# Linear attention and top-1 routing on one core: where the states grow, who zeroes the lists, when the early ranks are taken

## The chip, the cores and the metric

The kernel runs on one core of one Trainium2 chip. The metric is the device time in microseconds (us). A profile of one execution stands beside it; its times count from the start of that execution.

## What is computed

```python
for b in range(nb):                      # blocks of 64 positions
    intra = einsum('bhic,bhjc->bhij', qb, kb) * Dmask
    intra = einsum('bhij,bhjd->bhid', intra, vb)
    inter = einsum('bhid,bhde->bhie', qb * lam_pow, kv_state)
    out[:, :, sl] = intra + inter
    kv_state = lam_block * kv_state + einsum('bhsd,bhse->bhde', kb_dec, vb)
x = out.transpose(0, 2, 1, 3).reshape(B * S, H * D)          # 3072 x 512
expert_idx = argmax(x @ w_gate); gate_w = its softmax value
for e in range(8):
    out[mask] = gate_w[mask, None] * (relu(xe @ w1[e]) @ w2[e])
```

Batch is 4, heads 8, length 768, head size 64. Each of the 3072 tokens goes to one of 8 experts, with a hidden layer of 1024. Everything is float32.

## The kernel before

**Attention.** The kernel works in steps of 128 positions, so there are 6 steps n (`NSTEP`), and in each step it takes two batches b at a time. That makes 12 pairs, (0,0), (0,2), (1,0) and so on to (5,2), called pair 0 to pair 11 below. For a pair the following is done.

- `load` (L89) brings q, k and v of the pair by SyncE's queue. Each has a ring of three buffers. Pair 0 is loaded in halves, one batch at a time, with the decay rates `lam` behind q.
- `turn_qk` (L200) transposes q and k on PE in halves s of four heads (four transposes each for q and for k, in the order q, k, q, k). ScalarE copies the result into `qT` and `kT` (L212, L221). VectorE makes `qsT`, the decayed q, for n > 0, and GpSimd makes `kd`, the decayed k (L227).
- `score` (L232) multiplies `kT` and `qT`, and VectorE multiplies the result by the decay mask into `mt` (L243), one buffer for each half s, from a ring of two (pool `work`).
- `attend_states` (L254) adds what the states give, in two ways: way 0 before attention and way 1 after it. Between way 0 and attention stands the fence (L270): ScalarE copies one column of each of the two outputs, and attention, which adds to the same outputs, has to wait for that copy.
- `attend` (L272) multiplies `mt` and v into banks 6 and 7, 32 matmuls.
- `grow` (L286) multiplies `kd` and v into bank 4, 32 matmuls, for all steps but the last; `update` (L298) adds that to the decayed states.
- `to_sbuf` (L280) copies the outputs into `xT`. In the next iteration `rows` (L310) multiplies them by `back`, an identity with the gate weights beside it. That gives the tokens' rows, which go to the tensor `xs` in HBM, and their gate logits. It uses banks 4 to 7.

**Routing.** `choose` (L328) finds the expert of each token on VectorE. `put` (L360) ranks the tokens on PE (`rank`, bank 5) and GpSimd writes an entry for each token into the experts' lists `slots`, with one indirect write for each batch. Steps 0 to 3 are ranked four batches at a time, steps 4 and 5 two at a time. The lists have to be filled with empty entries first: GpSimd sets the tile `empty` (L383), which takes a buffer of the ring `mt`, and SyncE copies it into `slots` (L627), behind the loads of the first two pairs and eight small loads of the gate weights (L625).

Once batches 0 and 1 of step 4 are ranked, the first 256 places of expert 0's list are final, filled or left empty, and `start_early` (L673) reads them and gathers the rows. The ranks of these two batches are the early ranks. The first pass of the experts (`passes[0]`, list 0a) works on them. `turn` (L446) transposes the gathered rows in 8 transposes (L451); VectorE and ScalarE take turns in emptying the two banks that they use.

**Order.** `pin` (`keep_in_program_order`) keeps an instruction of PE where the program has it; what is not pinned is placed by a scheduler. The main loop (L691) has in each iteration: `leave` (rows and choice of the pair before), `enter` (loads and turn of the pair ahead), the ranks that are due from the iteration before, then this pair's states, attention, growth, second half of the states, and the scores of the pair ahead:

```python
        attend_states(cur, 0)
        attend(cur)
        grow(cur)
        attend_states(cur, 1)
```

After the loop come the transposes of the first pass, the last ranks, the last rows, and the experts: nine passes over lists, from the second on with fewer, larger products and sums on VectorE and GpSimd. The transposes of the first pass are not pinned, so they stand among the last pair's attention.

Of the kernel before, what the change touches and what calls it, by code (L numbers as in the profile page):

```python
# [10 lines left out]
F32 = mybir.dt.float32  # L11
I32 = mybir.dt.int32
# [8 lines left out]
def kernel(  # L21
# [64 lines left out]

    qkv = ctx.enter_context(tc.tile_pool(name="qkv", bufs=3))

    def load(n, b0, per=2, then=None):  # L89

        got = [qkv.tile([P, 2, H, D], F32, tag=name, name=f"{name}_in") for name in "qkv"]
        for t, src in zip(got, (q, k, v)):
            for b in range(0, 2, per):
                nc.sync.dma_start(
                    out=t[:, b:b + per].rearrange("p b h d -> p (b h) d"),
                    in_=src[b0 + b:b0 + b + per, :, n * C:(n + 1) * C, :].rearrange(
                        "b h s d -> s (b h) d"))
            if then and t is got[0]:
                then()
        return got  # L100


# [2 lines left out]
    def load_lam():  # L105
        nc.sync.dma_start(out=lam_bc, in_=lam.partition_broadcast(P))

    loaded = {(0, 0): load(0, 0, 1, load_lam), (0, 2): load(0, 2)}
    ident = const.tile([P, P], F32, name="ident")
    make_identity(nc, ident)  # L110

# [3 lines left out]
    for c in range(DC // 2):  # L115
        nc.gpsimd.tensor_copy(back[:, c, :P], ident)
        nc.gpsimd.tensor_copy(back[:, c, P + 2 * E:W + E + D], ident[:, D:])
        nc.gpsimd.tensor_copy(back[:, c, W + E + D:], ident[:, :D])
    before = const.tile([P, P], F32, name="before")
    make_upper_triangular(nc, before, val=1.0, diag=False)  # L120
    ones = const.tile([P, P], F32, name="ones")
# [67 lines left out]
    def bank(i, shape, name):  # L189
        return ps.tile(shape, F32, tag=f"bank{i}", name=name)  # L190
# [4 lines left out]

    pin = tc.keep_in_program_order

    def turn_qk(m, s):  # L200

        shp = [P, HP // 2, 2, C]

        def turned(src, t):
            for i, j in itertools.product(range(HP // 2), range(2)):
                h = s * HP + 2 * i
                pin(nc.tensor.transpose(t[:, i, j, :], src[:, j, h:h + 2, :], ident))  # L207
            return t

        tq = turned(m.q, bank(2 * s, shp, "tq"))  # L210
# [8 lines left out]
        tk = turned(m.k, bank(2 * s + 1, shp, "tk"))  # L219
# [31 lines left out]
    def out_at(m, b, u, hp):  # L251
        return m.op[b][halves[u ^ (hp & 1)], hp, :]

    def attend_states(m, way):  # L254

        if way == 0:
            m.op = [bank(6 + b, [P, HP, C], f"op{b}") for b in range(2)]
        if m.n > 0:
            for hp, b in itertools.product(range(HP), range(2)):
                u = b ^ way  # L260
                pin(nc.tensor.matmul(  # L261
                    out_at(m, b, u, hp), lhsT=st[halves[u], m.b + b, hp, :],
                    rhs=m.qsT[hp // 2][halves[u], hp % 2, b, :],
                    start=(way == 0 and hp < 2), stop=(way == 1 and hp >= HP - 2),
                    skip_group_check=True))
        if m.n > 0 and way == 0:


            for b in range(2):
                nc.scalar.copy(fence[halves[b ^ 1]], out_at(m, b, b, HP - 1)[:, C - 1:])  # L270

    def attend(m):  # L272
        for hp, b, u in itertools.product(range(HP), range(2), range(2)):
            pin(nc.tensor.matmul(  # L274
                out_at(m, b, u, hp), lhsT=m.v[:, b, 2 * hp + u, :],
                rhs=m.mt[hp // 2][:, u, hp % 2, b, :],
                start=(m.n == 0 and hp == 0), stop=(m.n == 0 and hp == HP - 1),
                skip_group_check=True))
# [81 lines left out]
    def put(n, bs, oh, ohc):  # L360


        nb = len(bs)
        shp = [P, nb, E]
        rank = bank(5, shp, "rank")
        pin(nc.tensor.matmul(rank, lhsT=before, rhs=oh, start=True, stop=False))  # L366
        pin(nc.tensor.matmul(rank, lhsT=ones, rhs=ohc, start=False, stop=True))
        place = small.tile(shp, F32, tag="place", name="place")
        nc.vector.tensor_add(place, rank, base[0].unsqueeze(1).to_broadcast(shp))
        nc.vector.tensor_mul(place, place, oh)  # L370
        slot = small.tile([P, nb], F32, tag="slot", name="slot")
        nc.vector.reduce_sum(slot, place, axis=AX.X)
        slot_i = small.tile([P, nb], I32, tag="slot_i", name="slot_i")
        nc.vector.tensor_copy(slot_i, slot)  # L374
        for i, b in enumerate(bs):
            put = nc.gpsimd.indirect_dma_start(  # L376
                out=slots, out_offset=bass.IndirectOffsetOnAxis(ap=slot_i[:, i:i + 1], axis=0),
                in_=entry[:, n, b, :], in_offset=None)

            tc.declare_no_dep(put.ins, group="put", reason="disjoint rows of the lists")  # L380
            tc.add_to_no_dep_group("put", put.ins)

    empty = work.tile([P, E * R // P, ENTRY], I32, tag="mt", name="empty")  # L383
    nc.gpsimd.memset(empty, 0)
    nc.gpsimd.memset(empty[:, :, 1], N)

# [56 lines left out]
        else:  # L443
            nc.vector.tensor_scalar_max(dst, src, 0.0)

    def turn(m):  # L446
        m.xgT = ffn.tile([P, DC, m.n], F32, tag="xgT", name="xgT", bufs=1)
        for dc in range(DC):
            tp = bank(next(tp_banks), [P, m.n], "tp")
            for t, w in enumerate(m.widths):  # L450
                nc.tensor.transpose(tp[:, t * P:t * P + w],  # L451
                                    m.xg[t // 2][:w, t % 2, dc * P:(dc + 1) * P], ident[:w, :w])
            evac(dc, m.xgT[:, dc, :], tp)

    def hidden(m, w1t):
# [163 lines left out]
                data1=zeros, initial=1.0, op0=ALU.mult, op1=ALU.add)  # L619
        nc.vector.tensor_copy(sdec[:, :, 0], qdec[:, :, C - 1])  # L620

    for c in range(DC // 2):
        for j, half in itertools.product(range(2), range(2)):
            f0 = (2 * c + j) * P + (half ^ j) * D
            nc.sync.dma_start(out=back[halves[half], c, P + j * E:P + (j + 1) * E],  # L625
                              in_=moe_w_gate[f0:f0 + D, :])
    nc.sync.dma_start(out=slots.rearrange("(p r) c -> p (r c)", p=P),  # L627
                      in_=empty.rearrange("p r c -> p (r c)").bitcast(F32))
    nc.sync.dma_start(out=xs[0, :].rearrange("(c p) -> c p", c=DC), in_=zeros[:DC, :])

    groups = ([(n, list(range(B))) for n in range(NSTEP - 2)]
              + [(n, [b, b + 1]) for n in range(NSTEP - 2, NSTEP) for b in range(0, B, 2)])
# [17 lines left out]

    def give_places(*group):
        put(*group)
        if group[:2] == early:
            start_early()
# [60 lines left out]


    cnt = bank(7, [P, E], "cnt")
# [121 lines left out]
```

## Time and profile before

The median of three runs is 502.1 us (500.6 to 502.86). The profiled execution has a span of 497.5 us.

| engine | busy us | share of the span |
|---|---|---|
| PE (matmul) | 465.9 | 94% |
| PEld (weight load) | 390.0 | 78% |
| VectorE (DVE) | 216.6 | 44% |
| ScalarE (ACT) | 129.5 | 26% |
| GpSimd (POOL) | 245.6 | 49% |

In the profile, L12 is line 12 of the kernel; a group's name reads output<-inputs. An entry in square brackets is the idle time of the engine before an instruction and what ended it. "PEclk" is the granted clock of PE in tenths. SPq, ACTq and POOLq are the queues from which SyncE, ScalarE and GpSimd issue transfers. Busy shares are averages over attention (to about 150 us) and the experts (the rest), which have different limits.

| load, from the issues | count | KB each | us to landing, median |
|---|---|---|---|
| q, k, v of a pair | 11 each | 512 | 7.8, 7.7, 9.0 |
| rows into `xs` | 24 | 256 | 4.6 |
| list entries into `slots` | 24 | | 4.3 |
| gather for list 0a | 2 | | 3.5 |

### The profile page before, as it was taken

Reading aid. Unit: us, or ns where it says so; the run is one execution under the profiler, and the core shown is the slowest. Engines: PE = TensorE matmul, PEld = TensorE weight load, DVE = VectorE, ACT = ScalarE, POOL = GpSimd, SP = SyncE. Lnnn points to the kernel's source line nnn. Section 1 sums busy time; section 2 is a strip of 40 time slices with the busy share of each in tenths; the row PEclk is TensorE's granted clock in tenths of the full one; section 3 lists DMA queues with packets and bytes.
Section 4 is the critical chain, followed back from the end, with each engine's and each line's share of the span. In section 5 each row is a group of like instructions: output and inputs, shape, how many; then the busy total and the mean of one; then the engine's idle time right before and its main releaser. Section 6 shows DMA issues by size and latency. Waiting matters only on the chain.

```text
span 497.5 us, 8717 instructions
## 1 busy us (share of the span) xinstructions
PE 465.9 (94%) x3468; PEld 390.0 (78%) x3468; DVE 216.6 (44%) x525; ACT 129.5 (26%) x333; POOL 245.6 (49%) x187
## 2 busy tenths in 40 slices
PE   5399999999969999999999999999999999999994
PEld 4398889889848657795799599589779879869963
DVE  2256565555624013446235524633723623563431
ACT  2144445444412011131212112222212211211210
POOL 5023545254233392985960992496298199531001
PEclk9689999999969999999999999999999999999999
DMA  9899998996121765706061542605326236001001
GB/s 186 163 233 260 226 278 234 300 260 153 46 85 44 253 196 180 260 25 237 28 211 32 202 145 93 233 24 212 131 118 215 90 144 210 22 19 42 1 16 49
DMA packets 99961, 72.85 MB, mean 146 GB/s; under 512 B 81266, under 2 KB 81270, under 8 KB 99912
## 3 DMA queue, kind: packets, MB, share of 16 engines
q1 hardware_dynamic: 91560, 52.96, 38.6%
q0 software_dynamic: 4896, 12.97, 7.2%
q10 hardware_dynamic: 3456, 6.29, 3.5%
q8 instruction: 29, 0.48, 0.4%
q14 instruction: 20, 0.16, 0.1%
HBM read 59.13 MB, written 13.40 MB: 146 GB/s over the span
## 4 chain that ended last, share of the span: by engine, by line
PE 69%; issue 1%; DMA 1%; DVE 1%; POOLq 0%; POOL 0%; ACT 0%
PE p L536 27%; PE p L564 17%; PE po L594 16%; PE ph L460 5%; PE tp L451 3%; DMA xg<-xs,list_0a 1%; PE op L274 1%; PE op L261 0%; DVE h_qsT L483 0%; DVE hT L545 0%; DMA slots<-entry,slot_i 0%; PE tx L316 0%; PE tx L318 0%; POOLq L792 0%; PE rank L366 0%
## 5 line engine op out<-in xcount | busy, mean ns | idle before, releaser
L594 PE MATMUL po<-w2t,hT 128*128 128x512 f32 (+2 forms) x224 | 81.1, 597 | 0.0
L422 POOL DMA_INDIRECT xg<-xs,list x24 | 25.9, 1080 | 75.4 <-PE tp L451 69.9
L594 PEld LDWEIGHTS po<-w2t,hT 128*128 128x128 f32 (+2 forms) x224 | 31.6, 169 | 37.5 <-issue 37.2
L547 ACT ACTIVATE hT<-hT 128x384 f32<-128x384 f32 (+2 forms) x56 | 30.2, 539 | 89.8 <-DVE hT L545 89.8
L428 POOL DMA_INDIRECT out_dram<-o,list x24 | 23.8, 990 | 52.0 <-DVE o L600 28.9
L376 POOL DMA_INDIRECT slots<-entry,slot_i x24 | 23.4, 976 | 46.9 <-DVE slot_i L374 21.6
L227 POOL TENSOR_TENSOR kd<-k_in,kdec 128x512 f32<-128x512 f32 x20 | 20.4, 1042 | 48.2 <-issue 26.3
L536 PE MATMUL p<-xgT,w1t 128*128 128x192 f32 (+2 forms) x224 | 42.8, 334 | 0.0
L536 PEld LDWEIGHTS p<-xgT,w1t 128*128 128x128 f32 x224 | 38.7, 190 | 1.1 <-issue 0.8
L243 DVE TENSOR_TENSOR mt<-sp,decay 128x512 f32<-128x512 f32 x48 | 30.0, 683 | 18.6 <-PE sp L237 10.0
L274 PE MATMUL op<-mt,v_in 128*64 128x128 f32 x384 | 25.9, 292 | 4.9 <-ACT fence L270 4.9
L274 PEld LDWEIGHTS op<-mt,v_in 128*64 128x64 f32 x384 | 23.0, 148 | 8.2 <-ACT fence L270 7.0
L576 DVE SCALAR_TENSOR_TENSOR o<-p,list,o 128x256 f32<-128x256 f32 x28 | 13.6, 484 | 32.9 <-PE p L564 17.0
L207 PE MATMUL tq<-ident,q_in 128*128 128x128 f32 x96 | 16.2, 294 | 12.0 <-DVE mt L243 7.3
L564 PE MATMUL p<-w2t,hT 128*128 128x256 f32 x112 | 26.8, 382 | 0.0
L564 PEld LDWEIGHTS p<-w2t,hT 128*128 128x128 f32 x112 | 21.0, 190 | 6.9 <-issue 4.4
L237 PE MATMUL sp<-qT,kT 64*128 64x128 f32 x384 | 26.3, 290 | 0.0
L451 PEld LDWEIGHTS tp<-ident,xg 128*128 128x128 f32 (+1 forms) x112 | 13.8, 144 | 15.2 <-issue 7.9
L237 PEld LDWEIGHTS sp<-qT,kT 64*128 64x128 f32 x384 | 24.0, 199 | 2.0 <-issue 1.5
L451 PE MATMUL tp<-ident,xg 128*128 128x128 f32 (+1 forms) x112 | 19.8, 288 | 5.8 <-DMA xg<-xs,list_0a 4.8
L460 PE MATMUL ph<-xgT,w1t 128*128 128x256 f32 (+1 forms) x128 | 24.7, 348 | 0.0
L545 DVE TENSOR_TENSOR hT<-p,u_qsT 128x384 f32<-128x384 f32 (+2 forms) x28 | 16.1, 575 | 16.5 <-PE p L536 16.5
(160 smaller groups left out, 946.1 us busy)
## 6 DMA issues: line engine op xcount, KB each, us to landing
w1t<-in_moe_w_dram SPq DMA_DIRECT2D x8, 2048.0 KB, 8.5
w2t<-in_moe_w_dram SPq DMA_DIRECT2D x8, 2048.0 KB, 8.8
xs<-x ACTq DMA_DIRECT2D x24, 256.0 KB, 4.6
q_in<-in_q_dram SPq DMA_DIRECT2D x11, 512.0 KB, 7.8
k_in<-in_k_dram SPq DMA_DIRECT2D x11, 512.0 KB, 7.7
v_in<-in_v_dram SPq DMA_DIRECT2D x11, 512.0 KB, 9.0
q_in<-in_q_dram SPq DMA_DIRECT2D x2, 256.0 KB, 3.5
k_in<-in_k_dram SPq DMA_DIRECT2D x2, 256.0 KB, 4.5
```

The costliest lines, as they stand in the source:

```text
L237: pin(nc.tensor.matmul(sp[u][:, i, b, :], lhsT=m.kT[s][halves[u], i, b, :], rhs=m.qT[s][halves[u], i, b, :], start=(i == 0 and b == 0), st ...
L243: nc.vector.tensor_mul(mt[:, u], sp[u], decay[:, u, s * HP // 2:(s + 1) * HP // 2].unsqueeze(2).to_broadcast(shp))
L274: pin(nc.tensor.matmul(out_at(m, b, u, hp), lhsT=m.v[:, b, 2 * hp + u, :], rhs=m.mt[hp // 2][:, u, hp % 2, b, :], start=(m.n == 0 and hp = ...
L376: put = nc.gpsimd.indirect_dma_start(out=slots, out_offset=bass.IndirectOffsetOnAxis(ap=slot_i[:, i:i + 1], axis=0), in_=entry[:, n, b, :] ...
L422: nc.gpsimd.indirect_dma_start(out=dst, out_offset=None, in_=xs[:rows, :], in_offset=bass.IndirectOffsetOnAxis(ap=idx, axis=0))
L428: put = nc.gpsimd.indirect_dma_start(out=out, out_offset=bass.IndirectOffsetOnAxis(ap=idx, axis=0), in_=src, in_offset=None, bounds_check= ...
L451: nc.tensor.transpose(tp[:, t * P:t * P + w], m.xg[t // 2][:w, t % 2, dc * P:(dc + 1) * P], ident[:w, :w])
L460: nc.tensor.matmul(ph, lhsT=w1t[:, dc, fc * P:(fc + 1) * P], rhs=m.xgT[:, dc, :], start=(dc == 0), stop=(dc == DC - 1))
L536: nc.tensor.matmul(p[:, i, :], lhsT=lhs[:, dc, (c + i) * P:(c + i + 1) * P], rhs=rhs[:, dc, :], start=(dc == 0), stop=(dc == DH - 1))
L547: nc.scalar.activation(outs[i][k], outs[i][k], ACT.Relu)
L564: nc.tensor.matmul(p, lhsT=lhs[:, fc, :], rhs=rhs[:, fc, :], start=(fc == 0), stop=(fc == FC // 2 - 1))
L594: nc.tensor.matmul(po[part], lhsT=m.hT[:, fc, t * P:t * P + w], rhs=w2t[:, fc, :], start=(i < k), stop=(i >= FC - k), skip_group_check=True)
```

## The change

It has five parts.

1. `grow` is called between the first half of the states and attention instead of after attention. It works on another bank, so that PE has something to do while the fence is awaited. The fence is now one column of one output, read by one copy.
2. `empty` moves to a buffer of its own, from the ring `xg`, which the experts use later. The copy into `slots` and the zero row of `xs` are issued by GpSimd instead of SyncE, and the gate weights come in four loads on ScalarE's queue instead of eight on SyncE's, at the start.
3. For pair 0, k is loaded on ScalarE's queue beside q on SyncE's, and the turn has both halves of q first and then both of k.
4. The early ranks are taken right after attention of pair 9, the pair whose iteration chooses them, instead of at the start of the states of pair 10.
5. The transposes of the first pass are pinned behind the last pair's states; the last ranks of all are no longer pinned.

```diff
-            for b in range(0, 2, per):
-                nc.sync.dma_start(
+            queue = nc.scalar if first and src is k else nc.sync
+            for b in range(0, 2, per):
+                queue.dma_start(
...
+    by_chunk = moe_w_gate.rearrange("(c j u d) e -> j u d c e", c=DC // 2, j=2, u=2)
+    for j, u in itertools.product(range(2), range(2)):
+        nc.scalar.dma_start(out=back[(u ^ j) * D:((u ^ j) + 1) * D, :, P + j * E:P + (j + 1) * E],
+                            in_=by_chunk[j, u])
...
-            for b in range(2):
-                nc.scalar.copy(fence[halves[b ^ 1]], out_at(m, b, b, HP - 1)[:, C - 1:])
+            nc.scalar.copy(fence[halves[0]], out_at(m, 1, 1, HP - 1)[:, C - 1:])
...
-        pin(nc.tensor.matmul(rank, lhsT=before, rhs=oh, start=True, stop=False))
-        pin(nc.tensor.matmul(rank, lhsT=ones, rhs=ohc, start=False, stop=True))
+        for lhs, rhs in ((before, oh), (ones, ohc)):
+            mm = nc.tensor.matmul(rank, lhsT=lhs, rhs=rhs, start=(lhs is before),
+                                  stop=(lhs is ones))
+
+            if (n, bs[-1]) != (NSTEP - 1, B - 1):
+                pin(mm)
...
-    empty = work.tile([P, E * R // P, ENTRY], I32, tag="mt", name="empty")
+    empty = ffn.tile([P, E * R // P, ENTRY], I32, tag="xg", name="empty", bufs=2)
...
-    for c in range(DC // 2):
-        for j, half in itertools.product(range(2), range(2)):
-            f0 = (2 * c + j) * P + (half ^ j) * D
-            nc.sync.dma_start(out=back[halves[half], c, P + j * E:P + (j + 1) * E],
-                              in_=moe_w_gate[f0:f0 + D, :])
-    nc.sync.dma_start(out=slots.rearrange("(p r) c -> p (r c)", p=P),
-                      in_=empty.rearrange("p r c -> p (r c)").bitcast(F32))
-    nc.sync.dma_start(out=xs[0, :].rearrange("(c p) -> c p", c=DC), in_=zeros[:DC, :])
+    nc.gpsimd.dma_start(out=slots.rearrange("(p r) c -> p (r c)", p=P),
+                        in_=empty.rearrange("p r c -> p (r c)").bitcast(F32))
+    nc.gpsimd.dma_start(out=xs[0, :].rearrange("(c p) -> c p", c=DC), in_=zeros[:DC, :])
...
-        for s in range(2):
-            turn_qk(m, s)
+
+        for s, turn_one in (((0, turn_q), (1, turn_q), (0, turn_k), (1, turn_k)) if not (n or b)
+                            else ((0, turn_q), (0, turn_k), (1, turn_q), (1, turn_k))):
+            turn_one(m, s)
...
         if due:
-            give_places(*due)
+            give_places(due)
         attend_states(cur, 0)
+        grow(cur)
         attend(cur)
-        grow(cur)
+        if chosen and chosen[0][:2] == early:
+            give_places(chosen.pop())
         attend_states(cur, 1)
...
-    turn(passes[0])
-    if chosen:
-        give_places(*chosen.pop())
+    turn(passes[0], pin)
+    give_places(chosen.pop())
     leave(last)
-    give_places(*chosen.pop())
+    give_places(chosen.pop())
```

More of the change, by code (lines that the diff above doesn't have):

```diff
@@ L87, with load @@
     qkv = ctx.enter_context(tc.tile_pool(name="qkv", bufs=3))
-    def load(n, b0, per=2, then=None):
+    def load(n, b0, first=False):
         got = [qkv.tile([P, 2, H, D], F32, tag=name, name=f"{name}_in") for name in "qkv"]
+        per = 1 if first else 2
         for t, src in zip(got, (q, k, v)):
+            queue = nc.scalar if first and src is k else nc.sync
             for b in range(0, 2, per):
-                nc.sync.dma_start(
+                queue.dma_start(
                     out=t[:, b:b + per].rearrange("p b h d -> p (b h) d"),
@@ L97, in load @@
                         "b h s d -> s (b h) d"))
-            if then and t is got[0]:
-                then()
+            if first and src is q:
+                load_lam()
         return got
@@ L106, in load_lam @@
         nc.sync.dma_start(out=lam_bc, in_=lam.partition_broadcast(P))
-    loaded = {(0, 0): load(0, 0, 1, load_lam), (0, 2): load(0, 2)}
+    loaded = {(0, 0): load(0, 0, True), (0, 2): load(0, 2)}
     ident = const.tile([P, P], F32, name="ident")
@@ L194, with pin, turned, turn_q @@
     halves = [slice(0, D), slice(D, P)]
[L198 to L210, printed above, removed]
+    def pin(inst):
+        tc.keep_in_program_order(inst)
+    turned_shape = [P, HP // 2, 2, C]
+    def turned(src, s, t):
+        for i, b in itertools.product(range(HP // 2), range(2)):
+            h = s * HP + 2 * i
+            pin(nc.tensor.transpose(t[:, i, b, :], src[:, b, h:h + 2, :], ident))
+        return t
+    def turn_q(m, s):
+        shp = turned_shape
+        tq = turned(m.q, s, bank(2 * s, shp, "tq"))
         qT = work.tile(shp, F32, tag="qT", name="qT")
@@ L218, in turn_qk, with turn_k @@
             m.qsT.append(qsT)
-        tk = turned(m.k, bank(2 * s + 1, shp, "tk"))
+    def turn_k(m, s):
+        shp = turned_shape
+        tk = turned(m.k, s, bank(2 * s + 1, shp, "tk"))
         kT = work.tile(shp, F32, tag="kT", name="kT")
@@ L444, in relu, with turn @@
             nc.vector.tensor_scalar_max(dst, src, 0.0)
-    def turn(m):
+    def turn(m, pin=lambda inst: inst):
         m.xgT = ffn.tile([P, DC, m.n], F32, tag="xgT", name="xgT", bufs=1)
@@ L450, in turn @@
             for t, w in enumerate(m.widths):
-                nc.tensor.transpose(tp[:, t * P:t * P + w],
-                                    m.xg[t // 2][:w, t % 2, dc * P:(dc + 1) * P], ident[:w, :w])
+                pin(nc.tensor.transpose(tp[:, t * P:t * P + w],
+                                        m.xg[t // 2][:w, t % 2, dc * P:(dc + 1) * P],
+                                        ident[:w, :w]))
             evac(dc, m.xgT[:, dc, :], tp)
@@ L644, in enter, with give_places @@
         m.q, m.k, m.v = loaded[n, b]
-        for s in range(2):
-            turn_qk(m, s)
+        for s, turn_one in (((0, turn_q), (1, turn_q), (0, turn_k), (1, turn_k)) if not (n or b)
+                            else ((0, turn_q), (0, turn_k), (1, turn_q), (1, turn_k))):
+            turn_one(m, s)
         return m
     chosen = []
-    def give_places(*group):
+    def give_places(group):
         put(*group)
```

## The prediction

> **What bounds the kernel now.** I read the busy tenths first, then PE's waits in the attention stage (0 to 160 us), then the timeline around each long wait, then the chain of waits, and last a table of stretches for the clock.
>
> ```profile
> PE   5399999999969999999999999999999999999994
> PEclk9689999999969999999999999999999999999999
> GB/s 186 163 233 260 226 278 234 300 260 153 46 85 44 253 196 180 260 25 237 28 211 32 202 145 93 233 24 212 131 118 215 90 144 210 22 19 42 1 16 49
> ```
>
> PE is full except in the first two slices (12.4 us each), the twelfth and the last; next to the first and in the twelfth the granted clock dips too. So it is attention, up to about 150 us, that has time to give. The waits (waiting engine and line, releaser: total us, times, longest):
>
> ```profile
> PE tq L207 <- DVE mt L243: 7.3, 1, 7.3
> PE op L274 <- ACT fence L270: 4.9, 9, 1.1
> PE tp L451 <- DMA xg<-xs,list_0a: 4.8, 2, 3.9
> DVE mt L243 <- DMA slots<-empty: 8.6, 1, 8.6
> ```
>
> The first and last are one wait. The timeline (start, us, instruction, idle before it) shows it:
>
> ```profile
> 12.24 6.83 SPq L625 DMA_DIRECT2D back<-in_moe_w_gate_dram  x8
> 19.19 0.52 SPq L627 DMA_DIRECT2D slots<-empty  x1
> 22.33 1.29 DVE L243 TENSOR_TENSOR mt<-sp,decay 128x512 f32<-128x512 f32 x2 [8.56 <-DMA slots<-empty]
> 23.08 1.11 PE L207 MATMUL tq<-ident,q_in 128*128 128x128 f32 x4 [7.30 <-DVE mt L243]
> 24.98 3.17 PE L274 MATMUL op<-mt,v_in 128*64 128x128 f32 x32
> 67.02 1.97 PE L274 MATMUL op<-mt,v_in 128*64 128x128 f32 x32 [1.06 <-ACT fence L270]
> 68.82 1.10 PE L291 MATMUL cp<-v_in,kd 128*64 128x64 f32 x32
> ```
>
> `empty` holds one of the two `mt` buffers until its copy into the lists lands, and that copy stands on SyncE's queue behind eight gate loads. The same 32 matmuls take 3.17 us after the pause and 1.97 in a later pair. The last two lines are the fence: PE waits for it between states and attention, with 1.1 us of growth matmuls standing behind.
>
> The chain of waits begins at the third hole:
>
> ```profile
> 131.98 0.96 DMA slots<-entry,slot_i
> 132.94 5.33 issue
> 138.26 0.28 POOL xg L422
> 138.55 1.00 issue
> 139.54 3.55 DMA xg<-xs,list_0a
> 143.13 0.90 PE tp L451 x3
> ```
>
> List entries, list read, gather, first transpose: 143.13 is set by how early the early ranks come. The stretches (length, busy us of PE, PEld, DVE, ACT, POOL, granted clock, DMA share, GB/s):
>
> ```profile
> 23.08:32.94 9.86, 9.86 (x120) 9.34 (x121) 4.31 (x11) 3.13 (x8) 2.04 (x2) 0.78 1.18 218
> 32.94:128.91 95.97, 91.36 (x1442) 84.76 (x1441) 56.28 (x170) 47.47 (x154) 40.03 (x40) 1.00 0.94 237
> 143.13:168.34 25.21, 25.20 (x162) 21.08 (x163) 9.35 (x57) 5.38 (x19) 7.75 (x9) 0.86 0.23 72
> 168.34:497.50 329.16, 321.32 (x1568) 259.68 (x1567) 136.06 (x242) 64.43 (x131) 185.56 (x108) 1.00 0.35 125
> ```
>
> The slow clock costs 9.86 x 0.22 = 2.2 us after the first hole and 25.21 x 0.14 = 3.5 us after the third. DMA is almost full during attention (0.94, 237 GB/s): there lies the danger.
>
> **What the Trainium skill says.** "TensorE: Matmul & The Clock Gate", Part 1: The HAM clock gate: PE falls to half clock after an idle window of about 3.4 us and needs as long a busy one to recover. The trace agrees (3.17 against 1.97 us, above). "DMA: Bandwidth & Descriptors", Issuing engines are not separate DMA queues: transfers from SyncE, ScalarE and GpSimd share the same engines; moving one saves only issue time. That is 6.83 us of issue here. "ScalarE: Activation LUTs", What ACT_TABLE_LOAD costs: 1283 ns; the trace has 1.28 us.
>
> **The change part by part.** Pairs are numbered 0 to 11.
>
> *Start.* `empty` leaves the `mt` ring, so the second product for pair 0 follows its scores. What then sets PE, step by step:
> - In the changed order ScalarE has two k loads, four gate loads and the table load ahead of its first copy; the third gate load waits for the first half of k, which PE had at 6.63. So the first copy starts at 6.6 + 2 x 0.6 + 1.3 = 9.1 instead of 6.05. Three copies of 0.59 later, at 10.9, the scores start (10.37 before), and end at 14.6 (3.69 us). Price of the move: 0.5 us.
> - Pair 1's k landed at 15.0. Now the zeros (432 KB, issued by GpSimd after its first `kd`, about 9.4 us) share the queue: pair 1's three loads of 0.52 MB landed at 12.6, 15.0 and 17.2, which is 230 GB/s, and 0.44 MB at that rate is 2 us; the earlier issue on SyncE returns about 0.5. So 16.5. No row shows a direct GpSimd copy; its issue lies between 1.0 us (the indirect rows) and 3 us (2.0 + 0.44/0.436, the DMA page's section Anatomy of one DMA, an estimate), and the second `kd` behind it is not due before 18. Hidden.
> - Then three quarter turns (0.6 each), growth 1.1, attention 1.9, scores 2.0, rows 1.95: pair 2's turn starts at 16.5 + 8.8 = 25.3. Its k must be there: pair 1's v at 17.2 + 2, two more loads of 2.25 us: 23.7. It is.
> - Before, that turn started at 32.94. Gain 7.6 (9 if the zeros disturb nothing, 5.6 if PE stays at the slow clock). It contains the 2.2 us of clock.
>
> *Growth between the halves.* Eight waits of pairs 2 to 9 sum to 4.6 us (0.26 to 1.06 each). The 1.1 us of growth now runs while ScalarE does the fence, now one copy, not two. Growth needs bank 4, which ScalarE empties before banks 6 and 7, which the states already await; and `kd`, which GpSimd finished a whole pair earlier even with four list writes (61.2 to 63.2, used at 68.8). Gain 4.4; 0.2 is left for hand-overs. Pairs 10 and 11 have no growth and keep their wait.
>
> *Early ranks in the same pair.* They move from 128.91 to behind attention of pair 9. Counted in times of before: turn of pair 10 ends at 118.35; ranks 0.5, states 0.6, growth 1.0, attention 1.8: about 122.5. Vector work puts the slots at 124, but GpSimd still issues the four writes of the group before (120.2 to 125.0), so the early two go at 125.0 to 127.3 instead of 130.71 to 132.94: 5.7 us earlier. List and gather follow as before: 137.4 instead of 143.1. The wait of `had` for VectorE (0.3) stays.
>
> *End pinned.* The transposes now stand behind the whole attention of pair 11. From 118.35 PE has 11.2 us to the end of pair 10's turn, 7.2 to the end of pair 10's rows, 3.7 for the last pair: it arrives at 140.5, 3 us after the rows. The 4.8 us of idling and the 3.5 us of slow clock go. Against that, nothing lies between the transposes any more: the third needs bank 0 back (0.4 us copy), the fourth a ScalarE copy behind two `xT` copies of 0.54: 0.7 us shown. The DMA is busier at that moment than before (list writes at 77 to 82 us landed after 5.8 us, idle ones after 2.1), so I take 0.5 us of waiting on average. Gain 4.8 + 3.5 - 0.7 - 0.5 = 7.1.
>
> *Moved along.* The other list writes in two pieces and the `xg` ring turned by one lie beside PE. The experts' 329 us run unchanged; the gather for the second pass landed at 173.4 and was used at 182: hidden as before.
>
> Sum: 7.6 + 4.4 + 7.1 = 19.1. 502.1 - 19.1 = 483.0.
>
> **The rivals.**
> - *The loads become the bound.* For it: 28.5 MB must land before the last attention (18.9 of q, k and v, 4.2 of weights, 5.0 of rows written, 0.4 of zeros). From 25 us on the seven full slices have 256 GB/s on average; with 5.2 MB landed by 26 the other 23.3 take 91 us, to 117; PE now wants the last pair about 12 us earlier (127.2 - 12 = 115). Against it: k and q of the last pair lie ahead of the second weight load, and before the change no pair after the second waited. If it came, half of start and fences (6) and 3 of the end would be lost: 492.
> - *The early list is late.* Writes and gather run into the last weight load, each landing 3 to 4 us later as above: about 8 us, PE pauses 5 us and cools again (3): 491.
> - *Slower.* Three queues cut each other down to, say, 200 GB/s (181 in the first stretch): 28.5/0.2 = 142 us, the last pair starts at 143 instead of 127.2; 16 lost, 7 gained at the end: 511.
>
> **How the numbers follow.** Forecast 0.75, loads 0.12, late list 0.08, slower 0.05. The likeliest gives 483. Its own bounds are 5.6 to 9 at the start, 4 to 4.6 for the fences, 4 to 8.3 at the end: 480 to 488.5. The range reaches down for a run or two of spread (500.6 to 502.86) and up to the two rivals: 477 to 491. Faster by over 0.5% (2.5 us) holds in all but the last case: 0.93; same 0.02.
>
> **What would show it.** No wait of a `mt` product for the zeros; pair 2's turn near 25; no fence wait over 0.1 us in pairs 2 to 9; early list writes right behind the four before them; transposes behind the last states, at 128 to 129, at full clock; the experts' stretch still 329 us. Wrong would be: PE waiting for q_in or k_in after pair 2, a gather landing after the last states, ScalarE's first copy after 10, or pair periods that stay at 10.6 us.

## The result and the profile after

| | median us | lowest to highest | runs |
|---|---|---|---|
| before | 501.72 | 500.60 to 502.86 | 4 |
| after | 478.49 | 477.37 to 478.98 | 4 |

The ratio is 0.9534, with a 95% interval of 0.9506 to 0.9562: 23.2 us or 4.6% faster. 483.0 was forecast, so the kernel gained 4 us more than the steps promised. The profiled execution of after has a span of 477.2 us (497.5 before), PE is busy for 457.3 us of it (465.9), 96%.

The busy tenths of after, as shown for before, 40 slices of the span:

```profile
PE   4799999999899999999999999999999999999994
PEclk9999999999999999999999999999999999999998
GB/s 170 240 243 260 217 239 216 257 305 279 101 47 320 157 193 250 32 243 33 208 13 242 36 212 87 157 199 47 243 110 132 233 39 211 0 19 44 1 17 51
```

The hole in the twelfth slice is gone, the second slice is fuller (7 for 3), and the granted clock no longer dips. The third row stays high without a break to the tenth slice and ends there: the last load of attention, pair 11's v, lands at 123.1 us.

PE's waits between 0 and 150 us (engine and line, releaser: us in all, times, longest):

```profile
PE tq L213 <- DMA q_in<-in_q_dram: 6.8, 2, 4.8
...
PE tp L465 <- DMA xg<-xs,list_0a: 1.3, 1, 1.3
PE tq L213 <- DVE mt L254: 1.1, 1, 1.1
PE op L284 <- ACT fence L280: 0.4, 2, 0.2
```

The first row is mostly the load of the very first q, 4.84 us, which before had too (4.17). The 7.3 us for an `mt` product are down to 1.1, and these are no longer a wait for zeros: VectorE's `mt` now waits for nothing but the scores. The ten fences cost 0.4 us in place of 4.9 (the two left are in pairs 10 and 11, which have no growth to put between), and the gather 1.3 in place of 4.8.

The start in the timeline of after (start, us, instruction, idle before it):

```profile
15.75 0.63 PE L213 MATMUL tk<-ident,k_in 128*128 128x128 f32 x4 [1.45 <-DMA k_in<-in_k_dram]
...
18.16 1.92 PE L284 MATMUL op<-mt,v_in 128*64 128x128 f32 x32
23.95 0.60 PE L213 MATMUL tq<-ident,q_in 128*128 128x128 f32 x4
```

Pair 1's k sets the pace at 15.75, as the prediction had it (16.5), and pair 2's turn, the last line, comes at 23.95 and not at 32.94. Attention of pair 0, the line between, takes 1.92 us, not 3.17: the clock stayed full through this wait and the 1.1 us before it.

The chain of waits that ended last begins, in after, with:

```profile
112.81 0.97 POOL slots L390
113.78 10.63 issue
...
125.70 3.79 DMA xg<-xs,list_0a
```

That is the same chain as before (list entries, list read, gather). The entry comes 19 us earlier (131.98) but the gather only 14 (139.54), since the line between them has grown from 5.33 to 10.63 us. We come back to it. What it costs PE is one entry of the timeline, at the transposes:

```profile
129.53 0.55 PE L465 MATMUL tp<-ident,xg 128*128 128x128 f32 x3 [1.27 <-DMA xg<-xs,list_0a]
```

And the stretches of after (length, busy us of PE, PEld, DVE, ACT, POOL, clock, DMA share, GB/s). They are pair 3's turn to the early ranks, and the experts:

```profile
33.06:108.45 75.39, 75.39 (x1234) 69.76 (x1232) 52.98 (x149) 37.29 (x119) 34.23 (x34) 1.00 1.02 248
...
148.08:477.20 329.12, 321.32 (x1569) 259.70 (x1567) 135.96 (x242) 64.51 (x131) 185.43 (x108) 1.00 0.35 125
```

In the first line PE is busy for all of its 75.39 us, where before had 4.6 us of fence waits in the like stretch. The last line is the experts' 329.16 us of before, untouched.

Cutting both traces at the same events (starts of turns, and the start of the first output product) tells where the 20.3 us between the two profiled spans came from:

| stretch | before | after | saved | forecast |
|---|---|---|---|---|
| start to pair 2's turn | 32.94 | 23.95 | 9.0 | 7.6 |
| pair 2's turn to pair 3's | 9.14 | 9.11 | 0.0 | in the next |
| pair 3's turn to pair 10's | 74.52 | 69.76 | 4.8 | 4.4 |
| pair 10's turn to the first output product | 51.57 | 45.10 | 6.5 | 7.1 |
| the rest | 329.30 | 329.27 | 0.0 | 0 |

The medians lie 23.2 us apart, 3 us more than these spans. The profiled execution of before took 499.25 us, 2.5 less than its median, and that of after 478.98, 0.5 more than its own. So some of what the change removes is probably larger in an ordinary execution of before than in the one profiled; the experiments below show which waits can vary.

### The profile page after: what moved, and what is told of

Same layout as the page of the kernel before. It is cut to its first block, busy times and chain, and to the rows that moved or that the text cites. A ratio compares the mean times of both kernels' runs of the same rounds, so it can differ in the third digit from the quotient of the medians.

```text
span 477.2 us, 8695 instructions
## 1 busy us (share of the span) xinstructions
PE 457.3 (96%) x3468; PEld 383.1 (80%) x3468; DVE 224.4 (47%) x525; ACT 127.0 (27%) x323; POOL 247.7 (52%) x189
## 4 chain that ended last, share of the span: by engine, by line
PE 71%; issue 3%; DVE 1%; DMA 1%; POOL 0%; POOLq 0%; ACT 0%
PE p L551 28%; PE p L579 18%; PE po L609 16%; PE ph L475 5%; PE tp L465 3%; DMA xg<-xs,list_0a 1%; DVE h_qsT L498 0%; DVE hT L560 0%; PE tx L326 0%; POOL slots L390 0%; PE tx L328 0%; DVE xgT L452 0%; PE rank L377 0%; POOLq L805 0%; ACT hT L562 0%
## 5 line engine op out<-in xcount | busy, mean ns | idle before, releaser
L390 POOL DMA_INDIRECT slots<-entry,slot_i x24 | 23.6, 985 | 34.9 <-DVE slot_i L388 13.7
L591 DVE SCALAR_TENSOR_TENSOR o<-p,list,o 128x256 f32<-128x256 f32 x28 | 13.5, 483 | 32.9 <-PE p L579 17.0
L248 PE MATMUL sp<-qT,kT 64*128 64x128 f32 x384 | 24.7, 278 | 0.1
L248 PEld LDWEIGHTS sp<-qT,kT 64*128 64x128 f32 x384 | 22.4, 188 | 2.2 <-issue 1.9
L284 PE MATMUL op<-mt,v_in 128*64 128x128 f32 x384 | 23.6, 274 | 0.4 <-ACT fence L280 0.4
L560 DVE TENSOR_TENSOR hT<-p,u_qsT 128x384 f32<-128x384 f32 (+2 forms) x28 | 16.1, 575 | 16.5 <-PE p L551 16.5
L293 ACT COPY xT<-op 128x512 f32<-128x512 f32 x24 | 12.9, 590 | 33.6 <-PE op L272 29.8
L488 DVE TENSOR_TENSOR u_kT<-p,u_qT 128x384 f32<-128x384 f32 (+2 forms) x14 | 8.1, 576 | 29.3 <-PE p L551 29.3
```

The source lines that it names most:

```text
L248: pin(nc.tensor.matmul(sp[u][:, i, b, :], lhsT=m.kT[s][halves[u], i, b, :], rhs=m.qT[s][halves[u], i, b, :], start=(i == 0 and b == 0), st ...
L284: pin(nc.tensor.matmul(out_at(m, b, u, hp), lhsT=m.v[:, b, 2 * hp + u, :], rhs=m.mt[hp // 2][:, u, hp % 2, b, :], start=(m.n == 0 and hp = ...
L390: put = nc.gpsimd.indirect_dma_start(out=slots, out_offset=bass.IndirectOffsetOnAxis(ap=slot_i[:, i:i + 1], axis=0), in_=entry[:, n, b, :] ...
```

## Experiments

**Theory.** The change is three separate savings at three places in attention, each about as large as its holes in the trace, and they add up. **Rivals.** The own buffer does all of the start and moving the queues nothing. Fences that vanish come back as waits for loads, which are full. At the end one of early ranks and pinning is idle, or the list writes behind the weight load take back what the early ranks win.

There were twelve runs, each with a profile. The first four stand beside the kernel before at 501.09 us (median of 7), the next four beside 513.57 (median of 11), on a chip where the same kernel takes longer, and the last four beside 501.33 (median of 11). Each is compared with its own kernel before; two kernels are compared with each other only within one of these groups.

### One part alone

**The buffer alone.** The kernel before with one line changed, so that the zeros get their own buffer but stay on SyncE's queue:

```diff
-    empty = work.tile([P, E * R // P, ENTRY], I32, tag="mt", name="empty")
+    empty = ffn.tile([P, E * R // P, ENTRY], I32, tag="xg", name="empty", bufs=2)
```

> The kernel before with one edit: the empty entries get their own buffer; SyncE still issues the gate loads and the zeros. If the queues matter too (my theory), PE's 7.3 us wait for the product goes, but the loads of pair 2 are still issued at 20.2 us behind the gate loads; its k lands at about 27, so pair 2's turn starts near 27.3 instead of 32.9: 5.6 us less than before. If the buffer was all (rival), the turn starts near 24 as in the changed kernel: 9 us less.

Measured: 495.71 us (494.00 to 496.63), ratio 0.9885 (0.9840 to 0.9931), 5.4 us faster. The timeline of this kernel shows where the rest of the start went:

```profile
20.92 0.39 SPq L94 DMA_DIRECT2D q_in<-in_q_dram  x1
25.69 0.63 PE L207 MATMUL tq<-ident,q_in 128*128 128x128 f32 x4 [2.05 <-DMA q_in<-in_q_dram]
28.51 1.09 PE L207 MATMUL tk<-ident,k_in 128*128 128x128 f32 x4 [2.19 <-DMA k_in<-in_k_dram]
```

Pair 2's loads now stand behind the eight gate loads, which SyncE issues from 12.50 to 19.81, and the zeros. Its q is issued at 20.92 and PE waits 2.05 us for it, then 2.19 for its k, and after that PE is at half clock (1.09 us for the four transposes instead of 0.63). Pair 3's turn comes at 38.06: 4.0 us earlier than before, where the whole change brings 9.0. So the wait for the buffer hid a second one behind it, that for loads that stand late in the queue.

**The whole start.** Parts 2 and 3 of the change, nothing else; beside the buffer, these lines:

```diff
-    for c in range(DC // 2):
-        for j, half in itertools.product(range(2), range(2)):
...
-    nc.sync.dma_start(out=slots.rearrange("(p r) c -> p (r c)", p=P),
+    nc.gpsimd.dma_start(out=slots.rearrange("(p r) c -> p (r c)", p=P),
...
+            queue = nc.scalar if first and src is k else nc.sync
...
+        nc.scalar.dma_start(out=back[(u ^ j) * D:((u ^ j) + 1) * D, :, P + j * E:P + (j + 1) * E],
```

> The kernel before with the whole start of the change (own buffer, zeros by GpSimd, gate weights and the first k on ScalarE's queue, all of q turned first) and nothing else. Theory, the parts add up: pair 2's turn at 24.0, 9.0 us less than before in time. Rival, the loads become the bound once PE is earlier: PE waits for q_in or k_in in later pairs and the gain is 6 us or less.

Measured: 492.28 us (489.73 to 494.29), ratio 0.9824 (0.9774 to 0.9874), 8.8 us faster. Pair 3's turn comes at 33.03, as in after (33.06). Of the 8.8 us the buffer alone had 5.4; the other 3.4 are the three moves between queues and the new order of the turn, taken together (the two kernels' intervals overlap a little; in the two profiles pair 3's turn lies 5.0 us apart). One of the moves is taken back by itself further down.

**Growth alone.** Part 1:

```diff
-            for b in range(2):
-                nc.scalar.copy(fence[halves[b ^ 1]], out_at(m, b, b, HP - 1)[:, C - 1:])
+            nc.scalar.copy(fence[halves[0]], out_at(m, 1, 1, HP - 1)[:, C - 1:])
...
         attend_states(cur, 0)
-        attend(cur)
         grow(cur)
+        attend(cur)
```

> The kernel before with growth between the first half of the states and attention, and one fence copy instead of two. Theory: PE's eight fence waits of pairs 2 to 9 (4.6 us) go and nothing takes their place: 4.5 us less. Rival: growth itself waits there for bank 4 or for the decayed k, and less than 2 us comes out.

Measured: 494.14 us (492.49 to 494.98), ratio 0.9837 (0.9789 to 0.9884), 7.0 us faster; the interval begins at 5.8. More than the 4.6 us of fence waits that the profile of before had to give. In its profile PE has no wait for a fence that the list of waits shows. The new order and the single copy were not tried apart; in pair 10, where no growth stands between, the wait for the shorter fence is 0.18 us in after, for 0.26 before, which suggests that most of the gain is the order.

**The end alone.** Parts 4 and 5:

```diff
+        if chosen and chosen[0][:2] == early:
+            give_places(*chosen.pop())
         attend_states(cur, 1)
...
-    turn(passes[0])
+    turn(passes[0], pin)
```

> The kernel before with the early ranks in the same pair and the first pass's transposes pinned behind the last attention. Theory: 4.8 us of waiting for the gather and 3.5 us of slow clock go, 0.7 us comes back between the transposes; the queue is empty there without the faster start, so list writes land in about 2 us: 7.6 us less. Rival, the clock stays slow there whatever the order: 4 us less.

Measured: 494.45 us (493.25 to 498.29), ratio 0.9838 (0.9793 to 0.9884), 6.6 us faster. PE waits for no gather any more (0.3 us for a copy of `xgT` is all that is left at the transposes).

The profiled execution of this kernel was its longest, 498.29 us, and it shows how a fence of the old order can cost far more than in the profile of before. Its timeline around the longest wait:

```profile
110.71 0.23 ACT L339 ACTIVATE ex<-sh 128x32 f32<-128x32 f32 x1 [2.39 <-DMA q_in<-in_q_dram]
...
112.62 3.68 PE L275 MATMUL op<-mt,v_in 128*64 128x128 f32 x32 [3.25 <-ACT fence L271]
```

ScalarE stands still for 2.39 us before it can issue the write of a block of rows into `xs` (at 110.33), and what releases it is the landing of a load of q that SyncE issued. Behind that write stand the exponential (the first line), three copies of the turn and the fence (112.41). PE waits 3.25 us for the fence and comes out of it at half clock (3.68 us for the 32 matmuls that take 1.97). That pair lasted 15.77 us, where 10.5 to 10.9 is usual.

So the fence of the old order can be drawn out by when a load happens to land. Its waits (us in all, times, longest) in the profiles with the old order, besides the 4.9 of before, are these: before on another chip, the buffer alone, the start alone, the end alone.

```profile
PE op L274 <- ACT fence L270: 4.5, 9, 0.7
PE op L274 <- ACT fence L270: 4.7, 9, 0.8
PE op L285 <- ACT fence L281: 6.5, 9, 1.8
PE op L275 <- ACT fence L271: 8.3, 10, 3.2
```

The five have a mean of 5.8. In the nine profiles with growth in between the sum is 1.3 at most, whatever the chip. But the forecast's 4.9 is the middle one of the five, and the two profiles of before itself lie 0.4 us apart; the two large sums belong to kernels whose other edits move the loads. That fences are longer in ordinary executions of before than in the profiled one is therefore possible and not shown, and what growth brings beyond the waits of the profile (7.0 for 4.6, or 5.8 at the near end of its interval) stays open.

The three parts give 8.8 + 7.0 + 6.6 = 22.4 us, the whole 23.2. They add up within the spread, which is about 2.4 us either way for each of them: none is seen to take from another, and no waits for loads came in place of the fences.

### The start's queues, one taken back

The kernel after, with k of pair 0 on SyncE's queue again (the order of the turn, both halves of q first, stays):

```diff
-            queue = nc.scalar if first and src is k else nc.sync
+            queue = nc.sync
```

> The kernel after with the k of pair 0 on SyncE's queue behind q, the rest of the start as in the kernel after. If the loads of q and k share one rate of transfer, all that is lost is the time in which k's issue stands behind q's two: 0.5 to 1.2 us for the first scores, and the kernel is slower by no more than that. If the second queue fetches k beside q, k lands 2 us or more later, and pair 2's turn moves by as much from 23.95.

Measured: 479.26 us (478.81 to 480.19; ratio to before 0.9553, 0.9517 to 0.9589), beside 477.35 (476.96 to 479.96) for the kernel after: 1.9 us slower, though the two ranges overlap. Neither reading had the way it went. The timeline of this kernel:

```profile
16.19 1.09 PE L213 MATMUL tk<-ident,k_in 128*128 128x128 f32 x4 [2.67 <-DMA k_in<-in_k_dram]
...
20.68 2.65 PE L284 MATMUL op<-mt,v_in 128*64 128x128 f32 x32
27.20 0.60 PE L213 MATMUL tq<-ident,q_in 128*128 128x128 f32 x4
```

and that of the kernel after, run beside it:

```profile
15.54 0.63 PE L213 MATMUL tk<-ident,k_in 128*128 128x128 f32 x4 [1.36 <-DMA k_in<-in_k_dram]
...
17.96 1.92 PE L284 MATMUL op<-mt,v_in 128*64 128x128 f32 x32
```

With one queue the first scores start 0.74 us earlier (9.68 for 10.42), since ScalarE has less to issue ahead of its first copy. But the wait for pair 1's k is one piece of 2.67 us instead of two of 0.68 and 1.36, and after it growth and attention run at half clock (1.98 and 2.65 us against 1.15 and 1.92). Pair 2's turn is 3.45 us later (27.20 for 23.75): 0.65 of it is the later k, 2.8 the slow clock. The Trainium skill ("TensorE: Matmul & The Clock Gate", Part 1: The HAM clock gate) gives an idle window of about 3.4 us for the fall; here one pause of 2.67 us was enough, after 9.45 us of which PE was busy for 7.84, and two shorter waits with transposes between them were not. The profiled execution of this kernel was its longest (480.19), and two of the six runs of the kernel after (479.64 and 479.96) were slower than its other three (478.81 to 479.32). So the 1.9 us are not clear of the spread, and that they are mostly the clock is what this one pair of traces shows. Why pair 1's k lands later was not tried by itself; in the trace the 432 KB of zeros are issued 2 us earlier than in after (9.89 against 11.89) and so run beside it.

### The end: early ranks, pinning, the weight load

Three kernels, each the kernel after with one edit, all on the chip where the kernel before takes 513.57 us. First, the early ranks a pair later, as they were:

```diff
         attend(cur)
-        if chosen and chosen[0][:2] == early:
-            give_places(chosen.pop())
```

> The changed kernel, but the early ranks again stand before the states of pair 10; the transposes stay pinned behind the last attention. Theory: the list entries are issued some 6 us later (117.6 instead of 111.5), the gather lands at 132 to 134 instead of 129.5, and PE, which is there at 127.9, waits 4 to 6 us instead of 1.3: 3 to 5 us more than the changed kernel, and up to 3 more if PE cools. Rival: the writes are held up by the last weight load either way, so the earlier ranks gain nothing: less than 1 us more.

Measured: 487.66 us (486.58 to 489.09), ratio to before 0.9517 (0.9485 to 0.9548).

Then the transposes of the first pass not pinned:

```diff
-    turn(passes[0], pin)
+    turn(passes[0])
```

> The changed kernel, but the first pass's transposes are not pinned, so that they stand ahead of the last pair's attention. Theory: PE reaches them at 124.0, waits for the gather to 129.5 and still has 3.9 us of attention to do, partly at the slow clock after 5.5 us of idling: 4 us more than the changed kernel without the clock, 7 with it; I expect 6.5. Rival: with the early ranks the gather is nearly there, the pin is worth under 1.5 us.

Measured: 487.35 us (485.36 to 488.50), ratio 0.9499 (0.9464 to 0.9535).

And the second weight load of the first expert issued behind the read of list 0a instead of ahead of the last pair's v:

```diff
-            weights.append(load_weights(0))
+            w1_first.append(load_w1(0))
...
+        weights.append((w1_first[0], load_w2(0, tc.keep_in_program_order)))
```

> The changed kernel with one move: the first load of the second weights is issued behind the read of the early list instead of ahead of the last v. Theory: the early list entries took up to 8 us to land because that load had the queue; without it they land in 3 to 4 us, the gather is there before 127.9, and PE's 1.3 us wait goes: 1.3 us less than the changed kernel. Rival: other loads and row writes hold the entries up, or the weights now come late for the first outputs at 148: no gain, or a loss.

Measured: 486.85 us (486.05 to 489.03), ratio 0.9494 (0.9467 to 0.9522).

The three lie within 0.8 us of each other, and their ratios about that of the kernel after. But the kernel before takes 513.57 us on this chip, 12 more than elsewhere, so it was profiled there as well:

> The kernel before, profiled once more. In the run of growth alone 7 us came out where the fence waits in the profile of before sum to 4.9. Theory: those waits differ from execution to execution, because ScalarE's row writes wait for loads to land and the fence stands behind them in ScalarE's queue; a second profile then has other fence waits, some over 1.1 us. Rival: the waits are the same again within 0.3 us in sum, and the 7 us came from elsewhere.

Measured: 511.86 us, span 510.1. Its waits have entries that the first profile of the same kernel lacks:

```profile
PE op L261 <- issue: 6.1, 10, 1.0
PE cp L291 <- issue: 1.5, 4, 0.4
```

"issue" is time in which PE waited for nothing that the trace shows. In the timeline the 16 matmuls of a second half of the states take 2.66 us (59.67 to 62.33), where the first profile has one entry of 0.67. The last piece of it:

```profile
61.85 0.48 PE L261 MATMUL op<-qsT,st 64*64 64x128 f32 x7 [0.97 <-issue]
```

Four pairs last 13.5 to 13.7 us in place of 10.5 to 10.9: 4 x 3 = 12 us, the whole difference (7.6 of them in the two waits above, the rest in matmuls that are drawn out). The fence, which this profile was taken for, does not bear the theory out: its waits sum to 4.5 us (4.9 in the first profile), and none is over 0.7.

In none of the three kernels on this chip does PE wait for the gather, since it reaches the transposes late (from 133.55, 136.91 and 137.63 on, where after has 127.93). So they could not tell what an earlier gather is worth. They do show a price of the early ranks. VectorE stands still for 5.5 to 5.6 us in all three, from 110.5 or 111.3 on, for something outside the trace ("remote"), and where the early ranks are taken in that pair, PE has to wait for it. In the kernel with the loose transposes:

```profile
115.97 0.17 DVE L383 TENSOR_TENSOR place<-rank,ebase 128x16 f32<-128x16 f32 x1 [5.48 <-remote]
116.20 0.60 PE L688 MATMUL had<-acc_early,ones 128*128 128x8 f32 x2 [3.51 <-DVE place L383]
117.79 3.69 PE L248 MATMUL sp<-qT,kT 64*128 64x128 f32 x32
```

`had` sums the tokens that each expert has so far and uses the bank of `rank`, so it waits until VectorE has read the ranks. The prediction left this wait at 0.3 us, which it is in the profiles of after; here it is 3.5, and the scores behind it run at half clock. With the ranks a pair later it is 0.27, though PE then has pauses of its own at that point.

Two of the three were run once more on another chip, with the kernel after beside them:

> The kernel after, as the reference beside the three kernels that follow. If the differences between parts don't depend on the chip, its ratio to the kernel before is 0.953 again, within 0.003. If the early ranks, the pinning and the place of the weight load are all worth something, it lies 2 us or more off the kernels with one of them undone; if none is, within 1 us of them.

Measured: 477.35 us (476.96 to 479.96), ratio 0.9535 (0.9501 to 0.9568), as the first time.

> The kernel after with the early ranks a pair later again, at the start of the states of pair 10. By the prediction's reading they bring the gather 5.7 us forward; the pinned transposes were reached 1.6 us before the gather was there, so without the early ranks they wait some 5 to 7 us more and the kernel is 5 to 7 us slower than the kernel after. Rival: the list writes are held up by the second weight load, and a pair later they land in an empty queue, in 2 instead of 8 us; then the kernel loses 1 us at most.

Measured: 478.67 us (477.77 to 481.61), ratio 0.9554 (0.9520 to 0.9588): 1.3 us slower than after, with ranges that overlap. Not 5 to 7. The issues of the early ranks' second write and of the list read, first in the kernel after, run beside it:

```profile
112.84 0.96 POOL L390 DMA_INDIRECT slots<-entry,slot_i  x1 [0.30 <-issue]
119.38 0.37 SPq L412 DMA_DIRECT2D list_0a<-slots  x1
```

and with the early ranks a pair later:

```profile
118.36 0.96 POOL L390 DMA_INDIRECT slots<-entry,slot_i  x1 [0.31 <-issue]
120.84 0.37 SPq L412 DMA_DIRECT2D list_0a<-slots  x1
```

The early ranks bring their writes 5.5 us forward (112.84 for 118.36), just as forecast (5.7). But the list read, which needs them landed, comes forward by 1.5 us at most (119.38 for 120.84), and with it the gather. The earlier two take 7.6 and 6.5 us to land, the later two 3.5 and 2.4. Until then the last loads drain: in the kernel after, the second weight load lands at 117.88 and the v of pair 11 at 120.74. Even the 1.5 us is not steady. In the first profile of after, the list read is issued at

```profile
120.70 0.37 SPq L412 DMA_DIRECT2D list_0a<-slots  x1
```

and the gather lands at 129.49, where the kernel with the later ranks has 129.36. PE waits 1.27 us for the gather there, not at all in the second profile, and 1.04 with the later ranks. By these profiles the early ranks gained between nothing and 1.5 us.

> The kernel after with the load of the first expert's second weights issued behind the read of list 0a. If the 8 us that the early list writes take to land come from that load, they land in 2 to 4 us, the wait of 1.3 us for the gather goes, and the kernel is 1 to 2 us faster than the kernel after. Rival: the weights then come too late for the second product of the first pass, and what is saved is lost there: no gain, or a loss.

Measured: 477.50 us (476.81 to 478.25), ratio 0.9521 (0.9493 to 0.9549): the kernel after within 0.2 us. The list read does come forward, from 119.38 to 116.86. But the weight load, issued right behind it at 117.28, now lies beside the gather, which is issued by 120.65 and lands at 127.89, where after has 128.02:

```profile
116.86 0.37 SPq L418 DMA_DIRECT2D list_0a<-slots  x1
117.28 0.46 SPq L188 DMA_DIRECT2D w2t<-in_moe_w_dram  x1
```

So the same megabytes stand before one step of the chain or the other. No version that was run beside the kernel after is faster than it.

The end can't be cut finer than that. Without early ranks the kernel loses 1.3 us in the medians, which is not clear of the spread, and without pinning nothing that shows on the chip where it was tried. It may be that either alone keeps the transposes from coming long before the gather, which is what cost 4.8 us of waiting and 3.5 of clock before the change; that is argued and not shown, since start and growth without both was not run.

## Why the prediction was right, point by point

**Start: right way, 1.4 us too small in the profile (9.0 for 7.6).** Pair 1's k did set the pace. Two terms were too large. Its k was taken for 16.5 and PE had it at 15.75. The 8.8 us from there to pair 2's turn took 8.2, since the three quarter turns, one behind the other, took 1.43 us for the 1.8 in the sum, and growth 0.98 for 1.1. The step on the first scores was wrong without consequence: ScalarE's first copy came at 8.16, not 9.1, and the scores ran at full clock (2.06 us for the 3.69 that were carried over from before), but PE then waited for k all the same. GpSimd's issue of the zeros, bounded between 1 and 3 us, took 0.66, below the bound; the upper figure is one for a whole transfer, and that took 4.74 us from issue to landing. What the Trainium skill says ("DMA: Bandwidth & Descriptors", Issuing engines are not separate DMA queues), that moving a transfer saves only the time in which it is issued, agrees with the runs, but that time was not small: with the buffer alone, eight gate loads hold SyncE's queue for 7.31 us, and pair 2's q, which PE needs soon, is issued behind them.

**Growth between the halves: right, undersized.** No fence wait of pairs 2 to 9 is left, and the profiles differ by 4.8 us, 4.4 forecast. In the runs it is 7.0, and 5.8 at the near end of the interval. The mis-sized term is "eight waits of pairs 2 to 9 sum to 4.6 us": it holds for the profiled execution and is less than the runs gain. That fences vary from one execution to the next would explain it and is not shown, as said above. By the runs of single parts growth brought 2.6 us more than forecast, the start 1.2 more (8.8 for 7.6) and the end 0.5 less (6.6 for 7.1): 3.3 of the 4.1 us that the change gained beyond its 19.1, the rest within the spread.

**Early ranks: the step was right and its worth was not.** "Early list writes right behind the four before them" came true (110.27, then 111.54 in the first profile of after), 5.5 us before those of the run that takes them a pair later. "List and gather follow as before" did not: the chain's second line took 10.63 us instead of 5.33. That was the rival of the late list, with its landing times of about 8 us; what it had too high is their price, 1.3 us in the first profile and nothing in the second in place of 5, and no fall of the clock, since PE got there at 127.93, just as the first half of the gather landed. So at this step the rival's mechanism came true and the forecast's did not. The total held because the forecast had the gather land 3 us before the transposes, and that room took up most of the delay.

**End pinned: 6.5 us in the first profile, 8.0 in the second, 7.1 forecast.** The waiting of 4.8 us and the 3.5 of slow clock both went. Against it stood 0.3 us for a copy, where 0.7 were taken, and 1.3 us for the gather in one run and none in the other, where 0.5 were taken. The prediction's arrival at the transposes, 128 to 129, is 127.93 and 127.96 in the two (the turn that ends its 11.2 us is pair 11's, not pair 10's). This is the joint result of parts 4 and 5; neither was found to be needed by itself.

**Loads and experts.** Neither the rival of the loads nor the slower one came. From pair 2 on PE waited 0.3 us for a load, while transfers ran at 248 GB/s from pair 3's turn to the early ranks (237 GB/s in the like stretch of before). The experts' 329 us did not move, as said.

## What to carry to other kernels

A profile shows one execution: for a wait that hangs on when a transfer lands, take its sum from several before you price its removal (the fence's lay between 4.5 and 8.3 us in five, and the list read moved by 1.3 us between two profiles of one kernel). When the longest wait goes, look what stands on the same queue behind it; here the own buffer gave 5.4 us and the rest of the start, queues and order of the turn, another 3.4. An earlier issue into a full DMA is worth only what its landing gains: 5.5 us of issue were at most 1.5 us of list read.

## What was not expected of the hardware

- ScalarE's issue of a row write waited 2.39 us for the landing of a load on another engine's queue, and all its later work with it; PE lost 3.25 us and then its clock. Why the write has to wait for that load the trace does not say.
- A single pause of 2.67 us halved the granted clock, while pauses of 1.10 and 1.45 us with 0.63 us of transposes between them left it full. In four pauses the clock fell 1.5 to 2.2 us after PE's last product (the first and third hole of before, the 3.25 us at the fence in the end alone, and this one); a pause of 2.05 us (the buffer alone) left it full. It was full again 2.9 us after PE's restart in the buffer alone, 4.4 after the first hole of before, 5.7 in the end alone and 6.0 here.
- The same kernel took 501.1, 501.3 and 513.6 us on three chips. The 12 us lie in PE's states and growth of every other pair, with pauses for which the trace names no releaser; in the three kernels made from after, VectorE, too, stood still on that chip for 5.5 us, for something outside the trace. The cause is open.
- An issue of a direct copy of 432 KB took GpSimd 0.66 us, less than the 1.0 of an indirect one.
